# Two attention blocks on one core: a second exponent shift that is the first done twice, and GpSimd instructions that carry one shift of each kind

## The chip, the core and the metric

The kernel runs on one NeuronCore of one Trainium2 chip. The core has five engines with a queue of instructions each: TensorE (PE, matmuls; PEld is its load of weights), VectorE (DVE), ScalarE (ACT), GpSimd (POOL) and SyncE (SP, which here only issues DMAs). Matmuls write PSUM, which GpSimd does not touch; everything else lies in SBUF. An engine takes its instructions strictly in the order in which the program wrote them, and waits where a semaphore of another engine, or its own, has not come far enough. The metric is the device time of one execution in microseconds, the median of several runs. An execution under the profiler has a time of its own and a span, from its first recorded instruction to its last.

## What is computed

Two attention layers over separate inputs of 2048 rows and 512 columns, with 32 heads of 16 each. A is linear attention, B is full softmax attention; their outputs stand side by side.

```python
q, k, v = qkv[0], qkv[1], qkv[2]            # x @ wqkv, split into 32 heads of 16
# A
pq, pk = phi(q), phi(k)                     # phi(t) = where(t > 0, t + 1, exp(t)) + 1e-6
kv = jnp.einsum("bhsd,bhse->bhde", pk, v)
num = jnp.einsum("bhqd,bhde->bhqe", pq, kv)
o = num / den
# B
scores = jnp.einsum("bhqd,bhkd->bhqk", q, k) * 16 ** -0.5
p = softmax(scores, axis=-1)
o = jnp.einsum("bhqk,bhkd->bhqd", p, v)
# both
out = concatenate([o_A @ wo_A, o_B @ wo_B], axis=-1)
```

B sets the time: 32 heads with 2048 by 2048 scores each, and an exponential of every one.

## The kernel before

**Blocks and units.** The scores of B are made in blocks of 128 keys by 512 queries. Four heads (g = 0 to 3) sit in the four 32-row groups of the array; a unit is one 512-query chunk for one parity of heads, so there are 32 units of 64 blocks, 2048 blocks in all. A block goes through a QK matmul into PSUM (`qk`, L862), an exponential, and a PV matmul (`pv_cand`, L1222) with V and a column of ones as the stationary operand, which gathers in the PSUM tile pPV. At the end of a unit VectorE transposes pPV (L1251), takes the reciprocal of the row sums (L1256), and GpSimd multiplies (L1257).

**Two ways to the exponential.** On the first way two or three blocks lie side by side in the tile pS, and one ScalarE instruction takes exp of 1024 or 1536 columns into the 25-block buffer PT (L1074); one PV matmul per block follows. Two such places in pS take turns. The PE rows that fill one are called a fill here. On the second way VectorE turns a block into an integer, score times ESC plus EB, rounded to int16 (L978, tile DI); these bits read as fp16 are a straight-line approximation of exp between powers of two. To smooth it, the same bits are used three times: as they are, plus `SHIFT[0]`, and plus `SHIFT[1]`. Three PV matmuls add the three patterns up, with the weights 1, 1 and VW: the third uses VX, a copy of V multiplied by VW (L675), in the place of V. A common factor drops out when a row is divided by its sum.

**The shifts.** Blocks of the second way are taken in groups of two, a buffer of DI for each of up to eight groups. When a group is complete (`chain`), each of its two shifts becomes one GpSimd instruction of 1024 columns (L1148). When a second shift with the same constant from another buffer is waiting as the first is taken up, both become one instruction of 2 by 1024 columns (`on_pool`). A second shift can also go to VectorE when GpSimd has much to do (L1132), and late ones in the last unit go to VectorE (L1154).

**Everything else** runs between: the projections of Q, K and V of B (L591, L668), all of A (L684 to L774), and the output projections (L800, and L1274 at the very end), whose results are cast into KNa (L573) and stored. The K projection of a later group of heads is cast into KR (L610) and then spread by eight DMAs on SP into KM (L615), four for the even heads and four for the odd ones, each with a semaphore of its own (s_d14 to s_d21).

**What sets the order.** A planner inside the kernel, which runs when the program is built, simulates the engines with fixed costs and picks one piece of work after the other; the instructions then stand in each queue in the order of its picks. The table SEG gives it 26 numbers per stretch of planned time: limits, lags and priorities, among them PMW, how long a GpSimd shift may be held back for a partner, and a noise and a seed with which equal candidates are shuffled. The dependency tracker `Sched.add` adds a semaphore wait where an instruction reads or overwrites what another one made, also where that one is on the same engine.

**A guard** bounds the scores from the inputs; when the bound is above THRESHOLD_BITS (read as a float, 1089), a general softmax follows. With these inputs it does not run.

Of the kernel before, what the change touches and what calls it, by code (L numbers as in the profile page):

```python
# [9 lines left out]
F16 = mybir.dt.float16  # L10
I16 = mybir.dt.int16
ACTF = mybir.ActivationFunctionType
ALU = mybir.AluOpType
# [110 lines left out]
THRESHOLD_BITS = 0x44882000  # L124
# [114 lines left out]
def bass_concat_heads__linear_attn_block__softmax_full_mha__prompt_kernel(nc, A_x, A_wqkv, A_wo, B_x, B_wqkv, B_wo, out):  # L239
# [17 lines left out]
    VW = 0.734375  # L257
    SHIFT = (336, 704)
# [95 lines left out]
    EB = 13476.7229  # L354
# [3 lines left out]
    with es:  # L358
# [601 lines left out]
        def d_emit(tk, en):  # L960
# [4 lines left out]
            for b, buf, bi in tk:  # L965
                def p1(st_, en_, buf=buf, bi=bi):
# [14 lines left out]
                    for x in bis:  # L981
                        b_ = waiting.pop(x)[1]
                        k_ = len(s_["items"])
                        s_["items"].append(b_)
                        dfree[x] = en_ + LPE["dve"]
                        pv_ready[b_[0]].append((en_ + LPE["dve"], b_, (DI.bitcast(F16)[:, buf, D0_ + k_ * 512:D0_ + (k_ + 1) * 512], ("DI", 0, buf, k_)), ("d", buf), "V"))
# [5 lines left out]
        pshift = []  # L992

# [116 lines left out]
        def chain(buf):  # L1110
# [10 lines left out]
            def give(buf_, v, lane, en_):  # L1121
                for i, b in enumerate(dgroup["st"][buf_]["items"]):
                    if lane == "dve":
                        P = gapped(DI.bitcast(F16)[:, buf_, :], DIV[v] + 33 + i * 528, 16, 32)
                    else:
                        P = DI.bitcast(F16)[:, buf_, DIV[v] + i * 512:DIV[v] + (i + 1) * 512]
                    pv_ready[b[0]].append((en_ + (PM if lane == "pool" else LPE["dve"]), b, (P, ("DI", v, buf_)), ("d", buf_), "VX"[v - 1]))
# [522 lines left out]
```

## Time and profile before

| what | value |
|---|---|
| time, 3 runs | 663.04, 663.52, 663.62 us; median 663.52 |
| time of the profiled execution | 663.59 us |
| its span | 661.9 us, 15921 instructions |
| busy PE, DVE, ACT, POOL | 635.4, 632.9, 646.1, 589.5 us |
| granted TensorE clock | 0.998 |
| DMA | 21.54 MB, 33 GB/s over the span |

Busy time says how long an engine had an instruction at work; two that overlap count once. In a row of a group of instructions stand the line, the engine, the operation, output and input tile, the shape, the count, then the busy time of the group and the mean duration of one, then the idle time before them and what ended it. A group of 587 with a mean of 1273 ns and 569.9 us busy is a group whose members overlap: each takes 1273 ns, but they start closer together than that. Durations of PE have modelled ends, so distances between starts are the better measure there. A row of the timeline or of the chain gives the start, the duration of the whole piece, and the number of instructions in it.

### The profile page before, as it was taken

The numbers are of one execution on the slowest core, as the hardware profiler recorded it, in microseconds if no ns is written. First come the engines' busy times: TensorE is split into PE (matmuls) and PEld (weight loads), VectorE is DVE, ScalarE is ACT, GpSimd is POOL, SyncE is SP. The second block draws the span as 40 slices with busy tenths as digits, with TensorE's granted clock in tenths as the row PEclk, the third lists the DMA queues.
The fourth block names the chain that finished last, engine by engine and source line by source line (L and its number), as shares of the span: only waits on it lengthen the run. The fifth ranks groups of instructions, "written<-read, shape, count | busy, mean of one in ns | idle before, by whom it ended". The sixth has DMA issues, their size and how long they took to land.

```text
span 661.9 us, 15921 instructions
## 1 busy us (share of the span) xinstructions
PE 635.4 (96%) x6603; PEld 201.5 (30%) x6658; DVE 632.9 (96%) x1065; ACT 646.1 (98%) x691; POOL 589.5 (89%) x493
## 2 busy tenths in 40 slices
PE   9999999999999999999999999999999999999996
PEld 6323332323323333323222223222222233222222
DVE  4999999999999999999999999999999999999985
ACT  6999999999999999999999999999999999999994
POOL 5989999998999998899989999899999999999981
PEclk9999999999999999999999999999999999999999
DMA  9701011010101101301002011100011000111011
GB/s 179 205 2 20 13 10 33 9 42 9 33 2 33 33 2 33 72 26 33 17 19 49 9 34 34 25 10 15 11 34 33 9 1 3 25 33 41 17 42 53
DMA packets 53214, 21.54 MB, mean 33 GB/s; under 512 B 44176, under 2 KB 52624, under 8 KB 53136
## 3 DMA queue, kind: packets, MB, share of 16 engines
q1 hardware_dynamic: 51664, 19.80, 13.4%
q8 instruction: 54, 0.88, 0.6%
q10 hardware_dynamic: 1472, 0.66, 0.4%
q14 instruction: 24, 0.20, 0.1%
HBM read 4.46 MB, written 4.19 MB: 13 GB/s over the span
## 4 chain that ended last, share of the span: by engine, by line
ACT 94%; PE 4%; DVE 1%; issue 0%; DMA 0%; DVEq 0%
ACT PT L1074 91%; ACT EA L684 2%; PE pD L800 1%; PE pPV L1222 1%; PE pS L862 1%; PE pD L1335 1%; DVE DI L978 0%; DMA out_dram<-KNa 0%; PE pS L1358 0%; DVE KNa L573 0%; PE pS L1274 0%; DVE DI L1154 0%; PE pS L800 0%; PE pS L1346 0%; PE pD L650 0%
## 5 line engine op out<-in xcount | busy, mean ns | idle before, releaser
L1074 ACT ACTIVATE PT<-pS 128x1024 f16<-128x1024 f32 (+1 forms) x653 | 639.0, 1312 | 1.0 <-PE pS L862 1.0
L1148 POOL TENSOR_SCALAR DI<-DI 128x1024 int16<-128x1024 int16 (+1 forms) x412 | 551.4, 1338 | 47.9 <-DVE DI L978 20.8
L978 DVE TENSOR_SCALAR DI<-pD 128x512 int16<-128x512 f32 (+1 forms) x463 | 324.5, 715 | 7.3 <-PE pD L862 3.9
L862 PE MATMUL pS<-QT,KM 32*128 32x512 bf16 x1555 | 256.8, 384 | 8.6 <-ACT PT L1074 3.4
L1222 PE MATMUL pPV<-PT,VV 128*17 128x512 f16 x1372 | 229.0, 381 | 0.0
L1222 PE MATMUL pPV<-DI,VV 128*17 128x512 f16 x1352 | 219.2, 381 | 0.2 <-DVE OT L1251 0.2
L862 PE MATMUL pD<-QT,KM 32*128 32x512 bf16 x493 | 168.7, 384 | 0.1
L1222 PE MATMUL pPV<-DI,VX 128*17 128x512 f16 x676 | 153.1, 384 | 0.0
L862 PEld LDWEIGHTS pS<-QT,KM 32*128 32x128 bf16 x1555 | 64.8, 90 | 263.7 <-ACT PT L1074 228.8
L978 DVE TENSOR_SCALAR DI<-pS 128x512 int16<-128x512 f32 x183 | 124.2, 679 | 1.1 <-PE pS L862 0.4
L1132 DVE TENSOR_SCALAR DI<-DI 128x1056 int16<-128x1056 int16 x118 | 80.6, 689 | 0.4
L1222 PEld LDWEIGHTS pPV<-PT,VV 128*17 128x17 bf16 x1372 | 47.7, 88 | 43.6 <-issue 37.8
L1222 PEld LDWEIGHTS pPV<-DI,VV 128*17 128x17 bf16 x1352 | 46.3, 88 | 40.6 <-issue 32.1
L862 PEld LDWEIGHTS pD<-QT,KM 32*128 32x128 bf16 x493 | 40.0, 91 | 5.2 <-DVE DI L978 2.5
L1222 PEld LDWEIGHTS pPV<-DI,VX 128*17 128x17 bf16 x676 | 32.8, 88 | 20.4 <-issue 17.0
L709 PE MATMUL pD<-Wa,xTa 128*128 128x256 bf16 x192 | 29.3, 275 | 0.0
L591 PE MATMUL pD<-xTb,Wb 128*128 128x512 bf16 x81 | 25.3, 382 | 3.3 <-issue 2.8
L1251 DVE STREAM_TRANSPOSE OT<-pPV 128x512 f32<-128x512 f32 x31 | 21.9, 707 | 0.1
L1257 POOL TENSOR_TENSOR OT<-OT,ZR 128x256 bf16<-128x256 f32 x31 | 19.2, 620 | 2.3 <-DVE ZR L1256 0.9
L684 ACT ACTIVATE EA<-pD 128x512 bf16<-128x512 f32 x22 | 18.6, 847 | 0.0
L709 PEld LDWEIGHTS pD<-Wa,xTa 128*128 128x128 bf16 x192 | 14.8, 97 | 12.5 <-issue 5.9
L573 DVE CAST KNa<-pD 128x512 bf16<-128x512 f32 x23 | 15.7, 682 | 2.1 <-PE pD L800 1.9
(145 smaller groups left out, 352.0 us busy)
## 6 DMA issues: line engine op xcount, KB each, us to landing
out_dram<-KNa SPq DMA_DIRECT2D x31, 128.0 KB, 1.7
Wa<-in_A_wqkv_dram SPq DMA_DIRECT2D x1, 1536.0 KB, 8.3
KM<-KR SPq DMA_DIRECT2D x96, 16.0 KB, 1.8
Wb<-in_B_wqkv_dram SPq DMA_DIRECT2D x2, 384.0 KB, 4.2
Wb<-in_B_wqkv_dram SPq DMA_DIRECT2D x1, 512.0 KB, 4.9
Wa<-in_A_wo_dram SPq DMA_DIRECT2D x1, 512.0 KB, 3.8
Wa<-in_B_wo_dram SPq DMA_DIRECT2D x1, 512.0 KB, 3.8
ON<-in_B_x_dram ACTq DMA_DIRECT2D x1, 256.0 KB, 2.8
```

The costliest lines, as they stand in the source:

```text
L573: return lambda e, bk: (e.tensor_copy(out_fn(), in_fn(bk)) if lane == "dve" else e.activation(out_fn(), in_fn(bk), ACTF.Copy))
L591: return e.matmul(f32v(bk), lhsT=Wb[:, cc, kind * 512 + Gp * 128:kind * 512 + Gp * 128 + 128], rhs=xTb[:, cc, sc * 512:(sc + 1) * 512], st ...
L684: ("act", 0.052 + n * 0.000833, f_ev("act", lambda e, bk: e.activation(EA[:, 0:n], f32v(bk)[:, c0:c0 + n], ACTF.Exp), [], ["EA"])),
L709: return e.matmul(f32v(bk)[:, 256 * tt:256 * tt + 256], lhsT=xTa[:, b, cc, (o + tt) * 128:(o + tt + 1) * 128], rhs=Wa[:, cc, 512 * kind + ...
L862: return e.matmul(dst, lhsT=KM[32 * g:32 * g + 32, Gp % 2, e_, j * 128:(j + 1) * 128], rhs=QT[32 * g:32 * g + 32, Gp % 2, c * 512:(c + 1) ...
L978: sch.add("dve", lambda e: e.tensor_scalar(DI[:, buf, D0_ + i * 512:D0_ + (i + n) * 512], f32v(DBANK[b0], n * 512), ESC, EB, op0=ALU.mult, ...
L1074: sch.add("act", lambda e: e.activation(PTf[:, p0 * 512:p0 * 512 + w], S5[:, c0:c0 + w], ACTF.Exp, scale=SC), reads=skeys(sl, len(bl)), wr ...
L1132: sch.add("dve", lambda e: e.tensor_scalar(gapped(DI[:, buf, :], DIV[v], wide // 32, 32), DI[:, buf, D0_ - 32:D0_ + w], 1.0, float(SHIFT[v ...
L1148: sch.add("pool", lambda e: e.tensor_scalar(DI[:, sl, DIV[v]:DIV[v] + w], DI[:, sl, D0_:D0_ + w], 1.0, float(SHIFT[v - 1]), op0=ALU.mult, ...
L1222: sch.add("pe", lambda e, g=g, j=j, c0=c0, V_=V_, r2=r2, P=P, first=first, last_=last_: e.matmul(PVb[32 * g:32 * g + 17, 0:512] if len(P.s ...
L1251: sch.add("dve", lambda e: e.transpose(OT[:, 0, :], PVb[:, 0:512]), reads=[("PV", g) for g in range(4)], writes=[("OT", 0)])
L1257: ("pool", 0.7, f_op("pool", lambda e: e.tensor_tensor(xn[:, :, 16 * e_:16 * e_ + 16], o[:, :, 0:16], zr.unsqueeze(2).broadcast_to([128, 1 ...
```

## The change

The second shift becomes twice the first one (328 and 656, before 336 and 704), so that a second shift may be made from the result of the first by adding the first constant again. The weights go with it: VW is 1.5546875, VX now multiplies the unshifted pattern, and V itself both shifted ones. EB and the guard's threshold (now 1024) follow.

GpSimd may now join two shifts of either kind: `on_pool` still prefers a partner with the same constant, but also takes one of the other kind from another buffer, if that buffer's own first shift is done by then. The joined instruction adds 328 to the plain pattern of one buffer and to the first shifted pattern of the other. It is written with an address pattern of two pieces. It waits on GpSimd's own semaphore, since its input was made there.

The table SEG is a new one throughout, and with it the order of all queues.

```diff
-    VW = 0.734375
-    SHIFT = (336, 704)
+    VW = 1.5546875
+    SHIFT = (328, 656)
+    PMX = 0.0
...
     SEG = (
-        (0.0,0.3,4,3.0,6,0,8,2,9.5,36,2.5,7.0,0.8,2.5,2,4.0,2.0,1.5,0.5,1,0,0.0,4,0,0,0),
...
+        (0.0,0.3,4,3.0,6,1,8,2,9.5,30,2.5,7.0,0.8,2.5,2,4.0,1.5,0.5,0.5,1,1,0.0,4,0,0,0),
...
-    EB = 13476.7229
+    EB = 13125.0
...
-                        pv_ready[b_[0]].append((en_ + LPE["dve"], b_, (DI.bitcast(F16)[...], ("DI", 0, buf, k_)), ("d", buf), "V"))
+                        pv_ready[b_[0]].append((en_ + LPE["dve"], b_, (DI.bitcast(F16)[...], ("DI", 0, buf, k_)), ("d", buf), "X"))
...
-                    pv_ready[b[0]].append((..., b, (P, ("DI", v, buf_)), ("d", buf_), "VX"[v - 1]))
+                    pv_ready[b[0]].append((..., b, (P, ("DI", v, buf_)), ("d", buf_), "V"))
...
                 def on_pool(st_, en_):
-                    two = [x for x in pshift if x[0] == v and x[2] == w and x[1] != buf and x[3][0] <= st_ + PMW]
+                    d1 = lambda b_: dgroup["st"][b_].get("v1", 1e9)
+                    two = [x for x in pshift if x[2] == w and x[1] != buf and x[3][0] <= st_ + PMW
+                           and (x[0] == v or d1(x[1] if v == 1 else buf) <= st_ + PMX)]
...
+                        if o[0] != v:
+                            st_ = max(st_, d1(o[1] if v == 1 else buf) - 0.03)
+                            keys = []
+                            for b_, v_ in segs:
+                                keys += [("DI", 1, b_)] if v_ == 2 else [("DI", 0, b_, i) for i in range(n)]
+                        else:
+                            keys += o[4]
                         T["pool"] = en_ = st_ + 0.276 + 2 * w * 0.00083
...
+                    mixed = len({v_ for _, v_ in segs}) == 2
...
+                    so = [b_ * pitch + (DIV[1] if mixed and v_ == 2 else D0_) for b_, v_ in segs]
+                    do = [b_ * pitch + DIV[v_] for b_, v_ in segs]
...
+                    sh_ = float(SHIFT[0] if mixed else SHIFT[v - 1])
+                    sch.add("pool", lambda e: e.tensor_scalar(dv, sv, 1.0, sh_, op0=ALU.mult, op1=ALU.add),
+                            reads=keys, writes=[("DI", v_, x) for x, v_ in segs])
```

What the built programs hold, counted in their queues: ScalarE has 587 exponentials of two blocks and 66 of three before, 582 and 69 after, so 1372 and 1371 blocks go the first way, 676 and 677 the second. GpSimd has 270 single and 142 joined shifts before (554 pieces), 236 and 160 after (556 pieces); 59 of the 160 hold one shift of each kind, and those 59 wait on GpSimd's own semaphore. VectorE makes 118 shifts in both. Line numbers move: QK is L858 after, PV L1241, the projections L587, the GpSimd shift L1164, the output projections L796 and L1293, the cast L569.

On GpSimd, early in the program, joined shifts stood among singles like this before (`128x2x1024` is a joined one, s_dve and s_pool are the semaphores of VectorE and of GpSimd itself):

```order
L1148 TENSOR_SCALAR DI<-DI 128x1024 [waits s_dve]
L1148 TENSOR_SCALAR DI<-DI 128x2x1024 [waits s_dve] x2
L1148 TENSOR_SCALAR DI<-DI 128x1024 [waits s_dve]
L1148 TENSOR_SCALAR DI<-DI 128x1024
L1148 TENSOR_SCALAR DI<-DI 128x2x1024 [waits s_dve]
```

and now, at about the same place:

```order
L1164 TENSOR_SCALAR DI<-DI 128x1024 [waits s_dve]
L1164 TENSOR_SCALAR DI<-DI 128x2x1024 [waits s_dve] x2
L1164 TENSOR_SCALAR DI<-DI 128x2x1024 [waits s_pool,s_dve]
L1164 TENSOR_SCALAR DI<-DI 128x1024 [waits s_dve]
```

Here a joined instruction has come in that waits on s_pool: it holds a first shift of one buffer and a second shift of another.

On PE, where Q and K of the third group of heads are projected, half way through the program, four projection matmuls (L591, tile Wb) stood between two fills (pS from QT and KM; the third pS row of an x3 can be a block of the second way) before:

```order
L862 MATMUL pS<-QT,KM 128x512 x3
L591 MATMUL pD<-xTb,Wb 128x512 x4
L862 MATMUL pS<-QT,KM 128x512 x2
L862 MATMUL pD<-QT,KM 128x512
L1222 MATMUL pPV<-PT,VV 17x512
L1222 MATMUL pPV<-DI,VV 17x512
```

and in the same stretch now:

```order
L858 MATMUL pS<-QT,KM 128x512 x3
L587 MATMUL pD<-xTb,Wb 128x512 x4
L1241 MATMUL pPV<-DI,VX 17x512 x2
L1241 MATMUL pPV<-PT,VV 17x512
L1241 MATMUL pPV<-DI,VV 17x512 x2
L1241 MATMUL pPV<-PT,VV 17x512 x3
L587 MATMUL pD<-xTb,Wb 128x512 x2
L858 MATMUL pS<-QT,KM 128x512 x2
```

Between the two fills now stand six projection matmuls and eight PV matmuls, where it was four projections. The fill that opens the piece is one of two blocks, and so are the one ahead of it and the one that closes it; the closing one also waits on s_d15, the second of the eight DMAs that spread K.

On VectorE at the very end, from the last shifts of the last unit to the end of its queue (L1312 and L1317 are the two transposes of each half of the last unit, L573 the casts of output tiles), before:

```order
L1154 TENSOR_SCALAR DI<-DI 128x1024 x2
L573 CAST KNa<-pD 128x512
L1312 STREAM_TRANSPOSE OT<-pPV 128x256
L1313 RECIPROCAL ZR<-OT 128x8
L1312 STREAM_TRANSPOSE OT<-pPV 128x256
L1317 STREAM_TRANSPOSE xTb<-OT 128x256
L1313 RECIPROCAL ZR<-OT 128x8
L573 CAST KNa<-pD 128x512
L1317 STREAM_TRANSPOSE xTb<-OT 128x256
L573 CAST KNa<-pS 128x512 x2
```

and now:

```order
L569 CAST KNa<-pD 128x512 x2
L1331 STREAM_TRANSPOSE OT<-pPV 128x256
L1332 RECIPROCAL ZR<-OT 128x8
L1331 STREAM_TRANSPOSE OT<-pPV 128x256
L569 CAST KNa<-pD 128x512
L1336 STREAM_TRANSPOSE xTb<-OT 128x256
L1332 RECIPROCAL ZR<-OT 128x8
L569 CAST KNa<-pD 128x512
L1336 STREAM_TRANSPOSE xTb<-OT 128x256
L569 CAST KNa<-pD 128x512
L569 CAST KNa<-pS 128x512
```

One more cast stands between the first transpose and the last one. On PE, 32 PV matmuls follow the last fill now, where it was four output matmuls and 17 PV matmuls; the run of PT matmuls that ends them has seven where it had three.

More of the change, by code (lines that the diff above doesn't have):

```diff
@@ L121, in emit_queue @@
             hook[1](eng)
-THRESHOLD_BITS = 0x44882000
+THRESHOLD_BITS = 0x44800000
 def _general_softmax(nc, es, ctx, sems):
@@ L985, in p1 @@
                         dfree[x] = en_ + LPE["dve"]
-                        pv_ready[b_[0]].append((en_ + LPE["dve"], b_, (DI.bitcast(F16)[:, buf, D0_ + k_ * 512:D0_ + (k_ + 1) * 512], ("DI", 0, buf, k_)), ("d", buf), "V"))
+                        pv_ready[b_[0]].append((en_ + LPE["dve"], b_, (DI.bitcast(F16)[:, buf, D0_ + k_ * 512:D0_ + (k_ + 1) * 512], ("DI", 0, buf, k_)), ("d", buf), "X"))
                     s_["t"] = en_
@@ L992, in bass_concat_heads__linear_attn_block__softmax_full_mha__prompt_kernel @@
         pshift = []
+        pv_give = {}
         def bank_at(at):
@@ L1126, in give @@
                         P = DI.bitcast(F16)[:, buf_, DIV[v] + i * 512:DIV[v] + (i + 1) * 512]
-                    pv_ready[b[0]].append((en_ + (PM if lane == "pool" else LPE["dve"]), b, (P, ("DI", v, buf_)), ("d", buf_), "VX"[v - 1]))
+                    pv_ready[b[0]].append((en_ + (PM if lane == "pool" else LPE["dve"]), b, (P, ("DI", v, buf_)), ("d", buf_), "V"))
             def shift(v, t_):
@@ L1136, in on_pool @@
                 def on_pool(st_, en_):
-                    two = [x for x in pshift if x[0] == v and x[2] == w and x[1] != buf and x[3][0] <= st_ + PMW]
+                    d1 = lambda b_: dgroup["st"][b_].get("v1", 1e9)
+                    two = [x for x in pshift if x[2] == w and x[1] != buf and x[3][0] <= st_ + PMW
+                           and (x[0] == v or d1(x[1] if v == 1 else buf) <= st_ + PMX)]
                     pshift.remove(me[0])
-                    bufs, keys = [buf], rk
+                    segs = [(buf, v)]
@@ L1140, in on_pool @@
+                    keys = list(rk)
                     if two:
-                        o = min(two, key=lambda x: x[3][2])
+                        o = min(two, key=lambda x: (x[0] != v, x[3][2]))
                         pshift.remove(o)
                         cands["pool"].remove(o[3])
-                        bufs, keys = sorted((buf, o[1])), rk + o[4]
+                        segs = sorted(segs + [(o[1], o[0])])
                         st_ = max(st_, o[3][0])
-                        T["pool"] = en_ = st_ + 0.276 + 2 * w * 0.00083
@@ L1147, in on_pool @@
-                    sl = slice(bufs[0], bufs[-1] + 1, max(bufs[-1] - bufs[0], 1))
-                    sch.add("pool", lambda e: e.tensor_scalar(DI[:, sl, DIV[v]:DIV[v] + w], DI[:, sl, D0_:D0_ + w], 1.0, float(SHIFT[v - 1]), op0=ALU.mult, op1=ALU.add),
-                            reads=keys, writes=[("DI", v, x) for x in bufs])
-                    for x in bufs:
-                        give(x, v, "pool", en_)
+                        if o[0] != v:
[5 more added lines that the diff above has]
+                            keys += o[4]
@@ new lines, in on_pool, with view @@
+                        T["pool"] = en_ = st_ + 0.276 + 2 * w * 0.00083
+                    mixed = len({v_ for _, v_ in segs}) == 2
+                    base = DI[:, segs[0][0], 0:1]
+                    pitch = DI[:, NDG - 1, 0:1].offset - DI[:, NDG - 2, 0:1].offset
+                    def view(offs):
+                        return bass.AP(base.tensor, DI[:, 0, 0:1].offset + offs[0], [list(base.ap[0])] + [[b_ - a_, 2] for a_, b_ in [offs] if len(offs) == 2] + [[1, w]])
+                    so = [b_ * pitch + (DIV[1] if mixed and v_ == 2 else D0_) for b_, v_ in segs]
@@ new lines, in on_pool @@
+                    do = [b_ * pitch + DIV[v_] for b_, v_ in segs]
+                    sv, dv = ([view(x) if len(x) == 2 else DI[:, segs[0][0], x[0] - segs[0][0] * pitch:x[0] - segs[0][0] * pitch + w] for x in (so, do)])
+                    sh_ = float(SHIFT[0] if mixed else SHIFT[v - 1])
+                    sch.add("pool", lambda e: e.tensor_scalar(dv, sv, 1.0, sh_, op0=ALU.mult, op1=ALU.add),
+                            reads=keys, writes=[("DI", v_, x) for x, v_ in segs])
+                    for x, v_ in segs:
+                        if v_ == 1:
+                            dgroup["st"][x]["v1"] = en_
+                        pv_give[x, v_](en_)
@@ L1152, in shift @@
+                pv_give[buf, v] = lambda en_: give(buf, v, "pool", en_)
                 if late:
```

89 rows, old and new, of the table SEG are left out of this document.

## The prediction

> **What bounds the kernel now.** I read the chain that ended last first, then the idle time of ScalarE, then the stretch between its first and last exponential.
>
> ```profile
> ACT 94%; PE 4%; DVE 1%; issue 0%; DMA 0%; DVEq 0%
> ACT KNa L573 <- PE pD L1274: 4.3, 1, 4.3
> ACT L483 <- issue: 2.3, 1, 2.3
> ACT xTb L573 <- PE pS L1346: 1.5, 1, 1.5
> ACT QT L1368 <- PE pS L1358: 1.3, 1, 1.3
> ACT PT L1074 <- PE pS L862: 1.0, 1, 1.0
> ...
> 8.68 21.98 ACT L1074 ACTIVATE PT<-pS 128x1536 f16<-128x1536 f32 x22 [1.05 <-PE pS L862]
> ...
> 8.68:651.21 642.53, 622.97 (x6512) 192.78 (x6565) 626.12 (x1045) 642.53 (x685) 581.31 (x466) 1.00 0.13 30
> ```
>
> ScalarE carries 94% of the chain. Its five waits lie at the two ends: four before or at the first exponential, which starts at 8.68 us, and one in the tail. The last row is the window from there to the end of the last exponential at 651.21 us (busy time with counts, for PE, PEld, DVE, ACT, POOL): ScalarE is busy for 642.53 of 642.53 us. So the time is three pieces: 8.7 us ahead of the first exponential, a ScalarE stretch without a hole, and 10.7 us of tail up to the span of 661.9. GpSimd, which the change works on, has 61 us of idle time inside the stretch. An engine with that much room sets the end only where something waits for it.
>
> **The price of one exponential.** The chain gives clean pieces.
>
> ```profile
> L1074 ACT ACTIVATE PT<-pS 128x1024 f16<-128x1024 f32 x587 | 569.9, 1273 | 0.0
> L1074 ACT ACTIVATE PT<-pS 128x1536 f16<-128x1536 f32 x66 | 109.2, 1654 | 1.0 <-PE pS L862 1.0
> ...
> 528.88 9.17 ACT PT L1074 x10
> 538.54 8.68 ACT PT L1074 x9
> ```
>
> Ten exponentials of two blocks take 9.17 us, 0.917 each. The next piece starts 538.54 - 538.05 = 0.49 later, which is one exponential of A between them (32 of these, L684). Its nine take 8.68, which is eight of 0.917 and one of three blocks, 1.344. Check: 587 x 0.917 + 66 x 1.344 + 32 x 0.49 = 642.7 against 642.53. The mean durations in the rows (1273 and 1654 ns) are longer than these distances because neighbours overlap; they are no price.
>
> **Term 1, ScalarE's work.** The change has 582 and 69: five fewer of 0.917, three more of 1.344, so -4.59 + 4.03 = -0.55 us. One block of 1372 has gone to the second way. Nothing else on ScalarE changes in number. With the stretch already full, this is all that the change can take out of it.
>
> **Term 2, what GpSimd saves.**
>
> ```profile
> L1148 POOL TENSOR_SCALAR DI<-DI 128x1024 int16<-128x1024 int16 x270 | 282.0, 1045 | 27.5 <-DVE DI L978 8.9
> L1148 POOL TENSOR_SCALAR DI<-DI 128x2048 int16<-128x2048 int16 x142 | 269.4, 1897 | 20.5 <-DVE DI L978 11.9
> L1222 PE MATMUL pPV<-DI,VV 128*17 128x512 f16 x1352 | 219.2, 381 | 0.2 <-DVE OT L1251 0.2
> ```
>
> 34 fewer singles are 34 x 1.045 = 35.5 us, 18 more joined ones 18 x 1.897 = 34.1: GpSimd gains 1.4 us of 589.5. On the path this is worth nothing: 48 us of its idle time stand ahead of these very rows, and the matmuls that read DI sit idle for 0.2 us in all. If that cover were gone, the whole 1.4 us would count. A joined instruction of two kinds has the same two pieces of 1024 elements as the joined ones of before, so I price it at 1.897; between bounds of 1.897 and two singles (2.09) it would cost GpSimd at most 59 x 0.19 = 11 us, still under the 61. Its wait on the own semaphore is seen in three tiny instructions that feed each other:
>
> ```profile
> 638.03 0.18 POOL L658 TENSOR_TENSOR TP<-TP 1x1 f32<-1x1 f32 x1
> 638.29 0.18 POOL L659 TENSOR_TENSOR TP<-TP 1x1 f32<-1x1 f32 x1
> ```
>
> The gap between them is 0.08 us; 59 such gaps are 4.7 us at most, also inside the room. Weights, SHIFT and EB change constants only: zero. VectorE evacuates 677 blocks for 676, one more of 0.68, with 626 of 642.5 us busy: hidden.
>
> **Term 3, one crowded place on PE.** I counted, in both orders, the PE work between each fill and the next, in rounds of 512 columns (a round is one projection matmul, up to four PV, or the up to four QK of one fill). Before, the largest is seven rounds, next to an exponential of three blocks. Now one place has nine: the place shown above in the third group's projections (1 QK, 4 + 2 projections, 8 PV = 2). Rows for a round:
>
> ```profile
> 651.58 1.47 PE L1274 MATMUL pS<-Wa,ON 128*128 128x512 bf16 x6
> ...
> 650.06 0.38 PE L800 MATMUL pD<-Wa,xTb 128*128 128x512 bf16 x1
> 650.37 0.38 PE L1222 MATMUL pPV<-DI,VV 128*17 128x512 f16 x1
> ```
>
> Six matmuls in 1.47 us, the last with 0.39 of its own, start (1.47 - 0.39) / 5 = 0.216 us apart; where the kind changes the distance is 0.31, so 0.09 more. The opening fill can start when an exponential has freed its place in pS. From then ScalarE holds two exponentials, 1.83 us. PE needs nine rounds, 1.94, then 0.38 until the closing fill's result, and four changes of kind, 0.36: 2.7 us with some 0.05 for semaphores. The hole is 0.9 us. Without the changes of kind it is 0.55; if two of the waits on VectorE in these rows (a free bank for each projection) cost one evacuation of 0.68 more, 1.6. I take 0.9, as the row with the change of kind is from the same matmuls. By the old order's largest place, 7 x 0.216 + 0.38 + 0.2 = 2.1 against 0.917 + 1.344 = 2.26, no hole, and none is in its trace.
>
> In the Trainium skill, the page "TensorE: Matmul & The Clock Gate", section "Back-to-back issue gap", gives a sustained spacing of 131 ns per matmul of 512 columns, and about 216 for an isolated one. By the 131 the nine rounds would be an estimated 1.2 us, the hole would close, and the sum would be 0.9 us lower. The trace does not agree: its 0.216 is the page's isolated figure, in a row of six.
>
> The closing fill also waits for the DMAs that spread K:
>
> ```profile
> KM<-KR SPq DMA_DIRECT2D x96, 16.0 KB, 1.8
> L615 SPq DMA_DIRECT2D KM<-KR x96: 507/588/1568, 106.2 to 503.9; - x96
> L610 DVE CAST KR<-pD x10: 674/680/692, 123.1 to 498.8; 128x512 bf16<-128x512 f32 x10
> DMA to landing us min/median/max: 1.7/1.8/3.5
> ```
>
> It waits for the second of eight: 0.59 + 1.8 = 2.4 us after the cast, at worst 1.57 + 3.5 = 5.1. Five fills stand between that projection's second half and the closing fill, 5 x 0.917 = 4.6 us, less a last round of 0.22 and the cast of 0.69: 3.7 us of cover, so this is hidden; at worst it makes the hole 1.4 us, in place of the 0.9 and not on top of it.
>
> **Term 4, the tail.**
>
> ```profile
> 651.69 0.45 DVE L1312 STREAM_TRANSPOSE OT<-pPV 128x256 f32<-128x256 f32 x1 [0.52 <-PE pPV L1222]
> ...
> 653.95 0.69 DVE L573 CAST KNa<-pD 128x512 bf16<-128x512 f32 x1 [0.52 <-PE pD L800]
> 654.56 0.43 DVE L1317 STREAM_TRANSPOSE xTb<-OT 128x256 bf16<-128x256 bf16 x1
> 655.68 1.48 DVE L573 CAST KNa<-pS 128x512 bf16<-128x512 f32 x2 [0.68 <-PE pS L1274]
> ```
>
> One more cast of 0.69 goes in ahead of the second L1317, but VectorE waited 0.52 there for PE, and now PE does those output tiles first after the PV matmuls: +0.17 remains. The PV matmuls that read the last exponentials are seven for three, one more round: +0.21. Together +0.4, between 0 (PE's four matmuls fewer between last fill and PV) and 0.9 (no cover at all).
>
> **Sum.** 663.59 - 0.55 + 0 + 0.9 + 0.4 = 664.3 us, against the profiled execution, which is 0.07 above the median; I let 664.3 stand. It is 0.1% above before. I call a difference under 0.2% (662.2 to 664.85) the same, about what a measurement of this kernel tells apart.
>
> **Rivals.**
>
> *The second pattern comes too late (slower).* A first shift that goes out in a joined instruction is done after 1.90 us and not after 1.05, so 0.85 later, and PE, which takes its queue in order, may stand on that PV with a fill behind it.
>
> ```profile
> PEld pS L862 <- ACT PT L1074: 228.8, 526, 0.7
> POOL DI L1148: 1.1, 5
> ```
>
> The cover is PE's wait for ScalarE ahead of a fill, 228.8 / 526 = 0.43 us; a hit makes a hole of 0.42 us. It decides from two hits in 59 on. Six hits give 664.3 + 2.5 = 666.8. Against it: waits of PV for GpSimd came to 1.1 us in five cases before, with 142 joined ones. 20%.
>
> *The crowded place costs more (slower).* If the two bank waits there each cost an evacuation, the hole is 0.9 + 1.36 and the time 665.7. For it: VectorE is busy 97% of the stretch. Against: it starts evacuations every 0.6 us, faster than fills come. 14%.
>
> *Only ScalarE counts.* If PE gets through the crowded place within ScalarE's supply, and the cast is hidden, 663.59 - 0.55 = 663.0: still the same by my bound. For it: the term rests on modelled ends of PE. Against: the 0.216 is a distance of starts. 18%. The Trainium skill's 131 ns, on the page named above, would have it so.
>
> *A shorter tail (faster).* PE no longer does four output matmuls (0.86 us) between the last fill and the PV matmuls. If the last round ends that much earlier and the hole is gone too: 663.0 - 0.86 = 662.1. Against it: the last PV waited for the last exponential. 6%.
>
> **How the numbers follow.** The forecast has the remaining 42%. Same: 42 + 18 = 60%; slower 20 + 14 = 34%; faster 6%. The range must leave out no more than 20%: it drops the faster case and the upper part of the late patterns and reaches from 662.8 to 666.2.
>
> **What would show it.** Right: the two-block exponentials still 0.917 apart; one idle row of ScalarE of 0.6 to 1.6 us near 338 us, released by a fill, and nothing else in the stretch; GpSimd busy about 588 us; the joined rows at about 1.9 us; an extra cast between the last transposes. Wrong: several holes in ScalarE that end with PE behind GpSimd's shifts (the first rival), a hole near 338 us behind VectorE (the second), none (the third), or a first exponential far from 8.7 us, which I took as unmoved because the rows ahead of it are the same.

## The result and the profile after

The changed kernel takes 664.70 us (median of 10 runs, 663.82 to 665.78), the kernel before 663.54 in the same series (10 runs, nine of them 663.01 to 663.63 and a stray one of 2791 us, which the ratio leaves out): a ratio of 1.002, with a 95% interval of 1.0011 to 1.0029. That is 1.2 us more, at the edge of what I had called the same. The profiled execution took 664.39 us, with a span of 662.3.

First the chain that ended last, by engine, in the changed kernel:

```profile
ACT 81%; PE 16%; DVE 1%; DMA 1%; issue 1%
```

Before, ScalarE had 94% of it and PE 4%. So the chain now leaves ScalarE somewhere in the middle and runs on PE for much of the way: 16% of 662 us are 106, some 44 of them between 293.65 and 340 us and some 60 from 589.5 us on, the tail included. The first of these stretches begins and ends so:

```profile
277.16 16.45 ACT PT L1071 x17
293.65 0.39 PE pS L858 x2
...
339.91 4.68 ACT PT L1071 x5
```

The idle time of ScalarE says what happens at 339.9 us:

```profile
ACT KNa L569 <- PE pS L1293: 5.0, 2, 4.5
ACT L479 <- issue: 2.3, 1, 2.3
ACT PT L1071 <- PE pS L858: 2.1, 2, 1.0
```

Total, times, longest. The third row was 1.0 in one piece before (the wait for the first exponential) and is 2.1 in two. The second piece is the hole; ScalarE's timeline shows it, and the end of the last exponential:

```profile
328.08 10.79 ACT L1071 ACTIVATE PT<-pS 128x1024 f16<-128x1024 f32 x11
339.90 4.69 ACT L1071 ACTIVATE PT<-pS 128x1024 f16<-128x1024 f32 x5 [1.02 <-PE pS L858]
...
633.31 18.46 ACT L1071 ACTIVATE PT<-pS 128x1536 f16<-128x1536 f32 x16
```

ScalarE stands from 338.87 to 339.90 and waits for a fill; the last exponential ends at 651.77, before at 651.21. Ahead of that and in that time PE does this. The 0.16 us in it are one matmul without a record; its weight load, at 338.93, has one.

```profile
337.10 0.39 PE L858 MATMUL pS<-QT,KM 32*128 32x512 bf16 x3
337.42 1.04 PE L587 MATMUL pD<-xTb,Wb 128*128 128x512 bf16 x4
338.39 0.39 PE L1241 MATMUL pPV<-DI,VX 128*17 128x512 f16 x2
...
338.61 0.39 PE L1241 MATMUL pPV<-PT,VV 128*17 128x512 f16 x3
339.16 0.38 PE L587 MATMUL pD<-xTb,Wb 128*128 128x512 bf16 x1 [0.16 <-issue]
339.47 0.39 PE L858 MATMUL pS<-QT,KM 32*128 32x512 bf16 x2
```

From the opening fill at 337.10 to the closing one at 339.47 it is 2.37 us; the closing fill's result comes 0.39 later. Nine rounds of 0.216 are 1.94, and four changes of kind make up the rest.

The tail, from the chain:

```profile
650.09 2.12 PE pPV L1241 x32
652.21 0.16 issue
652.37 1.89 PE pD L796 x8
654.26 0.65 PE pS L1293 x3
654.91 0.65 PE pD L1293 x3
655.55 0.86 PE pS L1293 x4
656.42 0.22 PE pD L1293
656.63 0.88 PE pS L1293 x4
657.51 0.02 issue
657.53 0.69 DVE KNa L569
```

Nothing but PE from the last PV matmuls to the last cast. (The matmul of 652.15 has no record; its weight load has one. So 24 matmuls stand behind the PV ones.) The last cast ends at 658.22, 6.46 us after the last exponential; before it was 657.16 - 651.21 = 5.95. And GpSimd's shifts:

```profile
L1164 POOL TENSOR_SCALAR DI<-DI 128x2048 int16<-128x2048 int16 x160 | 303.6, 1898 | 21.9 <-DVE DI L974 9.7 <-POOL DI L1164 2.9
L1164 POOL TENSOR_SCALAR DI<-DI 128x1024 int16<-128x1024 int16 x236 | 246.5, 1044 | 25.9 <-DVE DI L974 8.7
```

Joined instructions take 1.898 us whether they are of one kind or of two (all 160 lie between 1.897 and 1.902); the wait for the own result shows as 2.9 us in all.

So the difference is 643.11 - 642.53 = 0.58 us between the start of the first and the end of the last exponential and 0.51 behind that.

### The profile page after: what moved, and what is told of

Its sections match the earlier page's. It is cut to its first block, busy times and chain, and to the rows that moved or that the text cites. A ratio compares the mean times of both kernels' runs of the same rounds, so it can differ in the third digit from the quotient of the medians.

```text
span 662.3 us, 15966 instructions
## 1 busy us (share of the span) xinstructions
PE 634.0 (96%) x6597; PEld 201.2 (30%) x6652; DVE 633.6 (96%) x1074; ACT 645.7 (98%) x689; POOL 589.0 (89%) x477
## 4 chain that ended last, share of the span: by engine, by line
ACT 81%; PE 16%; DVE 1%; DMA 1%; issue 1%
ACT PT L1071 78%; PE pPV L1241 6%; PE pS L858 5%; ACT EA L680 2%; PE pD L796 2%; PE pD L587 1%; DVE DI L974 1%; DMA xTb<-in_B_x_dram 1%; PE pS L1293 0%; PE pD L858 0%; PE pD L742 0%; PE pS L1377 0%; DVE KNa L569 0%; PE pS L664 0%; PE pS L796 0%
## 5 line engine op out<-in xcount | busy, mean ns | idle before, releaser
L1164 POOL TENSOR_SCALAR DI<-DI 128x1024 int16<-128x1024 int16 (+1 forms) x396 | 550.1, 1389 | 47.8 <-DVE DI L974 18.4
L974 DVE TENSOR_SCALAR DI<-pD 128x512 int16<-128x512 f32 (+1 forms) x458 | 315.5, 705 | 7.8 <-PE pD L858 4.0
L858 PE MATMUL pS<-QT,KM 32*128 32x512 bf16 x1568 | 257.1, 384 | 9.0 <-ACT PT L1071 4.3
L1241 PE MATMUL pPV<-PT,VV 128*17 128x512 f16 x1371 | 232.6, 381 | 0.0
L1241 PE MATMUL pPV<-DI,VV 128*17 128x512 f16 x1354 | 225.6, 383 | 0.1
L858 PE MATMUL pD<-QT,KM 32*128 32x512 bf16 x480 | 164.2, 384 | 0.3 <-DVE DI L974 0.2
L1241 PE MATMUL pPV<-DI,VX 128*17 128x512 f16 x677 | 156.5, 382 | 0.0
L858 PEld LDWEIGHTS pS<-QT,KM 32*128 32x128 bf16 x1568 | 65.3, 91 | 261.0 <-ACT PT L1071 223.1
L974 DVE TENSOR_SCALAR DI<-pS 128x512 int16<-128x512 f32 x197 | 133.3, 677 | 0.8 <-PE pS L858 0.4
L1241 PEld LDWEIGHTS pPV<-PT,VV 128*17 128x17 bf16 x1371 | 48.3, 88 | 38.4 <-issue 32.3
L1241 PEld LDWEIGHTS pPV<-DI,VV 128*17 128x17 bf16 x1354 | 46.9, 88 | 42.9 <-issue 35.5
L858 PEld LDWEIGHTS pD<-QT,KM 32*128 32x128 bf16 x480 | 39.1, 91 | 7.8 <-DVE DI L974 4.0
L1241 PEld LDWEIGHTS pPV<-DI,VX 128*17 128x17 bf16 x677 | 33.7, 88 | 23.1 <-issue 21.0
L587 PE MATMUL pD<-xTb,Wb 128*128 128x512 bf16 x79 | 25.0, 383 | 3.7 <-issue 3.2
L705 PE MATMUL pD<-Wa,xTa 128*128 128x256 bf16 x160 | 24.4, 275 | 0.2 <-DVE DI L974 0.2
L680 ACT ACTIVATE EA<-pD 128x512 bf16<-128x512 f32 x27 | 22.5, 834 | 0.0
L569 DVE CAST KNa<-pD 128x512 bf16<-128x512 f32 x27 | 18.4, 680 | 2.6 <-PE pD L796 1.3
L742 PE MATMUL pD<-xTa,Wa 128*128 128x512 bf16 x51 | 15.9, 383 | 2.7 <-DVE DI L974 2.1
```

The lines of the kernel that those rows point to most:

```text
L569: return lambda e, bk: (e.tensor_copy(out_fn(), in_fn(bk)) if lane == "dve" else e.activation(out_fn(), in_fn(bk), ACTF.Copy))
L587: return e.matmul(f32v(bk), lhsT=Wb[:, cc, kind * 512 + Gp * 128:kind * 512 + Gp * 128 + 128], rhs=xTb[:, cc, sc * 512:(sc + 1) * 512], st ...
L680: ("act", 0.052 + n * 0.000833, f_ev("act", lambda e, bk: e.activation(EA[:, 0:n], f32v(bk)[:, c0:c0 + n], ACTF.Exp), [], ["EA"])),
L705: return e.matmul(f32v(bk)[:, 256 * tt:256 * tt + 256], lhsT=xTa[:, b, cc, (o + tt) * 128:(o + tt + 1) * 128], rhs=Wa[:, cc, 512 * kind + ...
L858: return e.matmul(dst, lhsT=KM[32 * g:32 * g + 32, Gp % 2, e_, j * 128:(j + 1) * 128], rhs=QT[32 * g:32 * g + 32, Gp % 2, c * 512:(c + 1) ...
L974: sch.add("dve", lambda e: e.tensor_scalar(DI[:, buf, D0_ + i * 512:D0_ + (i + n) * 512], f32v(DBANK[b0], n * 512), ESC, EB, op0=ALU.mult, ...
```

## The experiments

The schedule's calls are put in another order, or some are left out or replaced, just before the kernel is emitted; the waits are worked out anew from the new order. Line numbers are those of the changed kernel. Three stretches of the profiled execution tell more than one time, since the first exponential starts at 8.3 to 9.1 us and the last stores land at different moments from run to run. A hole is counted where the profile shows 0.15 us of idle time of ScalarE or more:

| kernel | first to last exponential | holes shown | last exponential to last cast | time, us (runs) |
|---|---|---|---|---|
| before | 642.53 | none | 5.95 | 663.44 (30) |
| changed, once more | 643.11 | 1.02 | 6.46 | 664.75 (11) |
| no_crowd | 643.16 | 0.27, 0.17 | 6.45 | 664.86 (11) |
| more_crowd | 643.54 | 1.46 | 6.45 | 665.37 (8) |
| fill_first | 643.21 | 0.58, 0.38 | 6.45 | 664.87 (11) |
| tail_casts | 643.11 | 1.03 | 6.46 | 665.69 (1) |
| tail_less | 643.11 | 1.02 | 5.62 | 665.17 (1) |
| split_two_kinds | 644.87 | 4, 2.0 in all | 6.52 | 666.70 (1) |
| split_one_kind | 652.17 | 12, 7.0 in all | 6.46 | 673.83 (1) |
| split_all | 663.24 | 25, 14.4 in all | 6.45 | 684.97 (1) |
| before_split_all | 659.44 | 21, 13.0 in all | 6.00 | 680.45 (1) |
| gpsimd_half | 643.11 | 1.03 | 6.45 | 664.96 (10) |
| eight_less | 642.69 | 0.49 | 5.62 | 663.77 (11) |

**after_again**, the yardstick.

> The changed kernel once more, as the yardstick for its neighbours on the same chip. Both theories: 664.7 us (663.8 to 665.4), span 662.3, one hole of 1.0 us in ScalarE near 339 us. If the 0.4 us by which time less span grew (1.7 before, 2.1 to 2.5 in the changed kernel) belongs to the kernel and not to the runs, it is seen again here.

664.75 us, ratio 1.0021 (1.0012 to 1.0030). The stretches repeat to 0.01 us, the hole is there. The time beyond the span was 1.7 to 1.8 us in all 30 runs of the kernel before and 2.1 to 2.6 in all 11 of this one.

**more_crowd.** On PE:

```diff
 L1241 MATMUL pPV<-PT,VV 17x512 x3
-L587 MATMUL pD<-xTb,Wb 128x512 x2
+L587 MATMUL pD<-xTb,Wb 128x512 x4
 L858 MATMUL pS<-QT,KM 128x512 x2
 L858 MATMUL pD<-QT,KM 128x512
 L858 MATMUL pS<-QT,KM 128x512 x3
-L587 MATMUL pD<-xTb,Wb 128x512 x2
```

> The second half of the same Q projection (two matmuls) goes ahead of the closing fill too, so that eleven rounds lie between the two fills. Theory (PE's rate): the hole grows by 2 x 0.216 = 0.43 to 1.45 us, and as the next stretch is two rounds lighter nothing is given back: +0.43, 665.1 us. Rival (a wait for VectorE's bank or for the DMAs sets the hole, PE has time to spare): the hole stays at 1.0 us, no change in time.

ScalarE's timeline:

```profile
339.93 4.69 ACT L1071 ACTIVATE PT<-pS 128x1024 f16<-128x1024 f32 x5 [1.46 <-PE pS L858]
```

Two rounds more, 0.44 us more hole, and 0.44 more to the last exponential (643.54). The hole is paid by the round: PE's rate sets it, not a wait for VectorE or a DMA. 665.37 us, ratio 1.0029 (1.0018 to 1.0040).

**fill_first.** The left-out rows are the eight PV matmuls.

```diff
 L587 MATMUL pD<-xTb,Wb 128x512 x4
+L858 MATMUL pS<-QT,KM 128x512 x2
...
 L587 MATMUL pD<-xTb,Wb 128x512 x2
-L858 MATMUL pS<-QT,KM 128x512 x2
 L858 MATMUL pD<-QT,KM 128x512
 L858 MATMUL pS<-QT,KM 128x512 x3
```

> Only the closing fill moves: it goes ahead of the eight PV matmuls and the half projection; no work is taken out. Theory (PE has hardly any time to spare in this whole stretch, 0.05 us a fill): the hole of 1.02 at the closing fill goes, but smaller ones, about 0.7 us together, open at the next two or three fills: 0.3 below the changed kernel, 664.4 us. Rival (the place is only badly ordered; PE has 0.43 us to spare ahead of every fill): no hole comes after it, 1.0 below, 663.7 us.

```profile
340.43 1.02 ACT L1071 ACTIVATE PT<-pS 128x1024 f16<-128x1024 f32 x1 [0.58 <-PE pS L858]
341.83 2.86 ACT L1071 ACTIVATE PT<-pS 128x1024 f16<-128x1024 f32 x3 [0.38 <-PE pD L858]
```

The hole moves to the next two fills, and 0.96 of 1.02 us comes back there. I had expected 0.7, and the rival none. PE has even less to spare than I thought: the place is not badly ordered, it has too much in it. The time is that of the changed kernel.

**no_crowd.** The first piece lies near 257 us, the others near 338, where the closing fill is also moved as in fill_first.

```diff
 L1241 MATMUL pPV<-PT,VV 17x512
+L587 MATMUL pD<-xTb,Wb 128x512 x4
 L858 MATMUL pS<-QT,KM 128x512 x2
...
-L587 MATMUL pD<-xTb,Wb 128x512 x2
...
-L587 MATMUL pD<-xTb,Wb 128x512 x2
```

> The crowded place is thinned: the third head-group's Q projection of the last 512 queries (four matmuls, one cast) goes to a place near 257 us with few rounds, and the closing fill goes ahead of the eight PV matmuls, so that five rounds lie between the two fills where there were nine. Theory (PE's rate: nine rounds at 0.216 us against two exponentials): the hole of 1.02 us near 339 us is gone, at most 0.2 us come back near 260 us where the four matmuls went; time 0.8 to 1.0 below the changed kernel, 663.8 us. Rival (the closing fill waits for VectorE's evacuations or for the DMAs that spread K, whatever PE has to do): 0.5 us or more of the hole stays, 664.2 or more.

```profile
259.06 17.95 ACT L1071 ACTIVATE PT<-pS 128x1024 f16<-128x1024 f32 x19 [0.27 <-PE pS L858]
...
343.38 1.02 ACT L1071 ACTIVATE PT<-pS 128x1024 f16<-128x1024 f32 x1 [0.17 <-PE pD L858]
```

The hole is gone and the time is not: 643.16, 664.86 us. My expectation failed. Near 259 us the four matmuls cost 0.5 us: the A exponential ahead of that place starts 0.23 us earlier than in the changed kernel (256.06 against 256.29), the next one 0.26 later (276.70 against 276.44). Near 338 us about 0.4 is gained, not 1.0, and this is what holds PE there now:

```profile
341.75 0.09 PEld L858 LDWEIGHTS pS<-QT,KM 32*128 32x128 bf16 x2 [0.43 <-issue]
342.09 0.09 PEld L858 LDWEIGHTS pS<-QT,KM 32*128 32x128 bf16 x1 [0.24 <-DVE DI L974]
```

The third QK matmul of that fill waits for VectorE to free its bank and starts 0.34 us after the first two, while VectorE does one piece after the other: evacuations, a transpose, a cast. With PE's crowd thinned, VectorE is the next to hold it. Here too, moving work moved the loss with it.

**tail_casts** and **tail_less** ask what sets the tail. VectorE in the first:

```diff
 L1331 STREAM_TRANSPOSE OT<-pPV 128x256
-L569 CAST KNa<-pD 128x512
 L1336 STREAM_TRANSPOSE xTb<-OT 128x256
 L1332 RECIPROCAL ZR<-OT 128x8
 L569 CAST KNa<-pD 128x512
 L1336 STREAM_TRANSPOSE xTb<-OT 128x256
-L569 CAST KNa<-pD 128x512
+L569 CAST KNa<-pD 128x512 x2
```

PE in the second:

```diff
-L796 MATMUL pD<-Wa,ON 128x512 x3
-L796 MATMUL pD<-Wa,xTb 128x512
```

> Only VectorE's order in the tail: the two casts of output tiles that lie between its transposes go behind the transposes they hold up (the first behind the second reciprocal, the second behind the last transpose). The prediction's step (the cast ahead of the second transpose costs 0.17 us): last cast 0.17 us or more nearer to the last exponential, 6.28 instead of 6.45. Rival (PE's queue of 24 matmuls sets the tail, the transposes have about 1.4 us to spare): 6.45 to 0.1.

> Left out: the four matmuls of one output tile of the tail (the first L796 tile after the last PV; its cast and store stay and write what the bank held), so that PE has 20 matmuls left after the PV ones as before the change. PE's queue sets the tail: last cast 4 x 0.216 = 0.86 us nearer to the last exponential, 5.6 us. Rival (VectorE's chain of transposes and casts sets it, as the prediction had it): 6.3 to 6.45.

tail_casts: 6.46, unchanged, although the last transpose now ends at 654.88 and not at 655.52. tail_less: 5.62, and the chain reads

```profile
652.69 0.16 issue
652.85 1.03 PE pD L796 x4
653.88 0.65 PE pS L1293 x3
...
657.17 0.69 DVE KNa L569
```

From the first matmul in the chain to the last cast it is 4.32 us, where the changed kernel has 657.53 - 652.37 = 5.16: 0.84 less, four times 0.21. PE's queue sets the tail. The single times of the two runs (665.69, 665.17) don't show it: the first exponential started at 8.59 and 9.14.

**split_two_kinds, split_one_kind, split_all, before_split_all.** One joined instruction becomes two in its place; written as an edit of that instruction, it is this:

```diff
-sch.add("pool", lambda e: e.tensor_scalar(dv, sv, 1.0, sh_, op0=ALU.mult, op1=ALU.add),
-        reads=keys, writes=[("DI", v_, x) for x, v_ in segs])
+for x, v_ in segs:
+    sch.add("pool", lambda e, x=x, v=v_: e.tensor_scalar(DI[:, x, DIV[v]:DIV[v] + 1024], DI[:, x, D0_:D0_ + 1024],
+                                                         1.0, float(SHIFT[v - 1]), op0=ALU.mult, op1=ALU.add),
+            reads=[("DI", 0, x, 0), ("DI", 0, x, 1)], writes=[("DI", v_, x)])
```

> The 59 shifts of two kinds in one instruction are each done as two GpSimd instructions again, in the same place of the queue, the second pattern from the plain one plus 656 (the same integers); nothing waits for a result of its own engine any more. Theory (GpSimd has room, its saving and its price are both worth nothing): GpSimd busy 589 + 59 x 0.19 = 600 us; from first to last exponential 643.1 us as in the changed kernel, to 0.2. Rival (a first shift that goes out with a second one comes 0.85 us too late and holds PE): shorter by 0.4 us for each hit, 642.3 or less.

> All 160 joined shifts, of one kind and of two, are done as two instructions each. GpSimd busy 589 + 160 x 0.19 = 619 us of the 643. Theory (room enough, as shifts are wanted late): first to last exponential 643.1 to 643.6 us. Rival (GpSimd near its limit queues its shifts up and PE stands on PV matmuls): 2 us or more longer, and idle time of PV ahead of GpSimd rises from 2.5 us to 5 or more.

My theory was wrong in both, by 1.76 and by 20 us; in split_two_kinds the rival was wrong too, and in split_all it was right. GpSimd was 599.8 us busy in the first, just as expected, and still the last exponential came 1.76 us later; with 617.4 us busy of a span of 682.8 it came 20 us later. PV's weight loads waited for GpSimd for 2.5 us in the changed kernel (10 times), 8.3 in split_two_kinds (25) and 29.0 in split_all (58). In split_two_kinds the chain runs on GpSimd alone for over 20 us up to the largest of the new holes, which is 0.58 us long and ends with the exponential of 105.67:

```profile
103.81 1.05 POOL DI L1164
...
104.91 0.39 PE pPV L1241 x2
105.30 0.32 PE pS L858 x2
...
105.67 1.01 ACT PT L1071
```

What I had taken for idle time is this (GpSimd's timeline in split_all, where L1602 are the split instructions, then in the changed kernel):

```profile
261.33 3.29 POOL L1602 TENSOR_SCALAR DI<-DI 128x1024 int16<-128x1024 int16 x3
```

```profile
100.90 2.17 POOL L1164 TENSOR_SCALAR DI<-DI 128x1024 int16<-128x1024 int16 x2
```

Three instructions of 1.045 us, one right behind the other, take 3.29, two take 2.17: between neighbours lie 0.08 us that no busy time counts and that no wait is named for. The Trainium skill, on the page "Perfetto Trace Analysis", section "GPSIMD Engine Instruction", says how to measure here: GpSimd's reported span is not to be relied on, and instructions are to be timed from start to start. The trace agrees, with 1.12 from start to start for a reported 1.045. The windows from first to last exponential (PE, PEld, DVE, ACT, POOL) of split_all and before_split_all, and the one of split_all from 60 to 640 us, show GpSimd at its limit:

```profile
8.77:672.01 663.24, 629.85 (x6503) 196.15 (x6555) 627.51 (x1053) 647.34 (x683) 609.08 (x609) 0.99 0.13 29
```

```profile
8.54:667.98 659.44, 630.09 (x6512) 196.51 (x6565) 626.55 (x1045) 646.00 (x685) 606.66 (x608) 0.99 0.13 29
```

```profile
60.00:640.00 580.00, 550.29 (x5724) 171.33 (x5767) 553.43 (x929) 566.24 (x603) 542.33 (x539) 1.00 0.10 23
```

(663.24 - 609.08) / 609 = 0.089 us per instruction, and 0.087 in the other; but these hold real waits for VectorE at both ends. Between 60 and 640 us it is (580.00 - 542.33) / 539 = 0.070: 0.08 between most shifts, 0.06 between some, and in 47 of 513 pairs of shifts the next one starts 0.036 us before the reported end. From the theory of 0.08 behind each instruction came the next two expectations.

> Only the 101 joined shifts of one kind are done as two instructions each; the 59 of two kinds stay joined. Theory (GpSimd's rate: each instruction takes 0.08 us beyond its busy time, 2.17 for two singles of 1.045 one behind the other; so 101 x (0.19 + 0.08) = 27 us more where 642.3 - 580.8 - 450 x 0.08 = 25.5 are free): 4 to 11 us longer than the changed kernel. Rival (GpSimd has room, and the 1.75 us of splitting the 59 came from the order of the two kinds): 1 us at most.

> The kernel before, with its 142 joined shifts done as two instructions each. Theory (GpSimd's rate, in any order of the work): 642.5 - 581.3 - 466 x 0.08 = 23.9 us are free, 142 x 0.27 = 38.3 are added: 14 to 20 us longer, 678 to 684 us; GpSimd without idle time but the 0.08 between instructions. Rival (only the changed kernel's order is so tight): 5 us at most.

9.1 us longer (652.17) and 16.9 longer (659.44): both inside their ranges, and the kernel before is just as tight as the changed one. At 0.27 us for each split, 27.3 us more work cost 9.1, 38.3 cost 16.9 and 43.2 cost 20.1. So about 20 us are free (18 to 23), and most of what goes beyond them is paid: 11.1 of the 15.9 us between split_one_kind and split_all. They are not free everywhere, since the 15.9 us of split_two_kinds already cost 1.76.

**gpsimd_half** asks for the other side. Input and output of each shift, joined or single, keep their starts:

```diff
-[[b_ - a_, 2], [1, 1024]]
+[[b_ - a_, 2], [1, 512]]
```

> Left out: the second 512 of every 1024 elements in 208 single and 146 joined shifts of the changed kernel (all but those of the first 75 us or so and the first use of each buffer); order and waits stay. GpSimd gets 208 x 0.42 + 146 x 0.85 = 210 us lighter. Theory (a faster GpSimd is worth nothing, since ScalarE's stretch is full but for PE's crowded place): first to last exponential 643.1 us to 0.2, the hole of 1.0 near 339 us stays, time as the changed kernel. Rival (late shifts cost the changed kernel something that the records of the waits hide, as splitting them cost 1.75 us): 642.6 or less.

GpSimd's busy time in the stretch fell from 581 to 368 us:

```profile
9.06:652.17 643.11, 620.83 (x6503) 192.21 (x6555) 626.46 (x1053) 642.08 (x683) 368.34 (x448) 1.00 0.13 30
```

and ScalarE's stretch is 643.11, to the hundredth that of the changed kernel, with the hole of 1.03. More than a third less GpSimd work buys nothing; 2% more, 10.8 of 589 us, cost 1.76.

**eight_less.**

```diff
-L587 MATMUL pD<-xTb,Wb 128x512 x2
-L587 MATMUL pD<-xTb,Wb 128x512 x2
-L796 MATMUL pD<-Wa,ON 128x512 x3
-L796 MATMUL pD<-Wa,xTb 128x512
```

> Left out: eight matmuls of the changed kernel, the four of the Q projection in and behind the crowded place (its cast stays) and the four of one output tile in the tail. Theory (PE's rate sets the hole and the tail, and these two are the whole of what the changed kernel lost): the hole shrinks by 2 x 0.216 + 0.09 to 0.5 us, first to last exponential 642.6; last cast 5.6 us behind the last exponential; together 1.35 us off 664.75, so 663.4 us, the time of the kernel before. Rival (the loss lies outside the span, where the changed kernel takes 0.5 us longer): the stretches shrink but the time stays at 664.2 or more.

```profile
339.27 1.94 ACT L1071 ACTIVATE PT<-pS 128x1024 f16<-128x1024 f32 x2 [0.49 <-PE pS L858]
```

The hole is 0.49, the tail 5.62, the time 663.77: ratio 1.0008 (0.9999 to 1.0017), where the changed kernel had 1.0021 on the same footing. The stretches are 1.26 us shorter, the median 0.98. The time beyond the span stays at 2.3 us in the median. So the loss is where PE has these matmuls, and the rival falls.

No version came out of this that beats both: each order that I tried with the whole of the work was level with the changed kernel or behind it.

## Why the prediction was right, and where it was not

**The bound** was right. ScalarE's stretch stayed full but for one hole. Full by busy time is not the same as fastest, though: an exponential of two blocks lasts 1.27 us, so one that starts a little late leaves no idle time. In the kernel before, the starts of two such neighbours lie 0.904 us apart in the median and 1.14 at most, by the starts in its trace. The reading of GpSimd was wrong: of the "61 us of idle time", 466 x 0.070 = 33 lie between instructions, and of the other 28 only about 17 lie between 60 and 640 us (580.00 - 533.21 us busy - 419 x 0.070).

**Term 1** was right: -0.55 said; 643.11 - 1.02 - 642.53 = -0.44 measured. This charges the hole with its idle time alone; only the sum of terms 1 and 3 is measured as such, 0.58 where 0.35 was said.

**Term 2** gave the right zero with half of the reason. The joined instruction of two kinds costs 1.898 us, as taken, and a lighter GpSimd is worth nothing (gpsimd_half). But the bounds were wrong. What I wrote of a higher price, "at most 59 x 0.19 = 11 us, still under the 61", would have been hidden by my account; split_two_kinds put 10.8 us there and lost 1.76. And the gap of 0.08 us, which I quoted from two tiny instructions and put down to the wait for the own result, stands behind most GpSimd instructions, whether or not one needs the other's result. Had two kinds not been joined at the price of one, this term would have made the forecast wrong.

**Term 3** was right in place, cause and size: one hole near 338 us, released by a fill, 0.9 said and 1.02 measured, and 0.22 us more for each further round. The rows of PE above have no wait for a bank, and none has the closing fill waiting for a K spread. The spacing of 131 ns, which the Trainium skill gives on "TensorE: Matmul & The Clock Gate" in "Back-to-back issue gap", would have left a hole of an estimated 0.1 us by the prediction's own sum (1.18 + 0.38 + 0.36 + 0.05 - 1.83), and not quite closed it; the four L587 matmuls in 1.04 us, (1.04 - 0.39) / 3 = 0.217 apart, do not agree with it. What the term did not see is that neither of the two other orders tried mends the place: fill_first and no_crowd paid the same elsewhere.

**Term 4** had the size, 0.4 for 0.51, by the wrong mechanism, so that it came near is luck. The failed steps are "One more cast of 0.69 goes in ahead of the second L1317" with its 0.17, and "one more round: +0.21". The cast costs nothing (tail_casts). The further round doesn't show: the first matmul behind the PV ones starts 0.37 us after the last exponential in both kernels, 651.58 - 651.21 before, and now at about 652.15, just behind its weight load:

```profile
652.14 0.10 PEld L1293 LDWEIGHTS pS<-Wa,ON 128*128 128x128 bf16 x1 [0.23 <-issue]
```

In their place stand PE's 24 matmuls where there were 20, 4 x 0.216 = 0.86 us, which tail_less gives back. Of these the kernel before had hidden 0.39. Its chain ends as in the first piece; the second is VectorE's cast ahead of that last one:

```profile
654.56 0.11 DVE xTb L1317
654.67 1.70 DMA out_dram<-KNa
656.37 0.03 issue
...
656.46 0.69 DVE KNa L573
```

```profile
655.68 0.69 DVE L573 CAST KNa<-pS 128x512 bf16<-128x512 f32 x1 [0.68 <-PE pS L1274]
```

Its last cast started at 656.46, when PE's last result had stood for 0.39 us (651.58 + 19 x 0.216 + 0.38 = 656.07). The chain puts this down to a store that landed at 656.37, but VectorE was busy with the cast ahead of it until 656.37 too, so which of the two held it stays open. Now it starts as soon as PE is done (657.51). 0.86 - 0.39 = 0.47 of the 0.51. I had counted the four matmuls that moved behind the PV only as a possible gain ahead of it.

**The sum** was 664.3 and the median 664.70. The stretches grew by 1.1 us and not by 0.75, about a tenth in each of terms 1, 3 and 4; what is left lies in the start, in the last stores and behind the span.

**The rivals.** *The second pattern comes too late*: PV matmuls waited for GpSimd 10 times for 2.5 us, and no hole came of it; with GpSimd a third lighter the stretch is the same. Its cover was misread, though: the 0.42 us ahead of a fill is no room.

```profile
337.10 0.10 PEld L858 LDWEIGHTS pS<-QT,KM 32*128 32x128 bf16 x3 [0.47 <-ACT PT L1071]
...
339.47 0.10 PEld L858 LDWEIGHTS pS<-QT,KM 32*128 32x128 bf16 x2 [0.42 <-issue]
```

The closing fill, for which ScalarE was standing idle, shows 0.42 where the opening one shows 0.47. It is the way of a change of kind, and only what goes beyond it is a wait. *The crowded place costs more* did not happen: the projections' weight load at 337.42 names VectorE, but starts 0.32 us after the fill, which is a change of kind and no more. Its mechanism, VectorE's bank, showed as soon as the place was thinned. *Only ScalarE counts* is refuted by the hole. *A shorter tail* is refuted with its sign: four matmuls that no longer stand ahead of the PV matmuls stand behind them.

## What to carry to other kernels

The idle time of an engine is room only after the gaps between its instructions are taken off: count instructions times what the start-to-start distance has beyond the reported duration. Where several engines are nearly full, price both directions: here a GpSimd that was a third lighter was worth nothing, and one with 27 us or more of added work was paid for most of what went beyond some 20. The cost of a crowded place was its rounds beyond two exponentials, and the other orders tried only moved it. In a tail, count what each queue still has to do after the last wait, and look for the chain through the queue that has no gap.

## What was not expected of the hardware

Most GpSimd instructions took 0.08 us beyond their reported time, 0.070 in the mean with the engine at its limit (539 instructions of split_all), beside a fixed part of its reported time of about 0.19 us: 0.621 us for 512 elements in gpsimd_half, 1.044 for 1024, 1.898 for 2 x 1024. The time between the end of the span and the end of the measured execution was 1.7 to 1.9 us in every run of the kernel before, and 2.1 to 2.6 in every run of the changed kernel and of those of its variants that were timed in rounds, also where 210 us of GpSimd's work or eight matmuls were left out. In the profiled executions of the two, the span ends 4.04 us after the last cast and not 4.70, but in the variants that is 3.9 to 5.1. What makes this difference stays open.
